# Attention, routing and a mixture of experts on one core: expert 0's first weights loaded and halved earlier, routing marks dealt anew

## Chip, core and metric

The kernel runs on one core of one Trainium2 chip. The metric is the device time of one execution in microseconds (us), the median of several. The core's engines are TensorE (PE for matmuls, PEld for weight loads), VectorE (DVE), ScalarE (ACT), GpSimd (POOL) and SyncE (SP), which here only issues DMAs.

## What is computed

Attention over 4 batches, 8 heads, 768 positions and 64 dimensions, where a query sees the first 8 positions and the last 96; then a layer of 8 experts in which each of the 3072 tokens goes to its best two.

```python
scores = scale * q @ k.T + bias            # bias: -slope * distance
scores = where(keep, scores, -1e9)         # keep: first 8 keys, or 0 <= distance < 96
a = exp(scores - max) / (sum + 1e-9);  x = (a @ v) as 3072 tokens x 512
noisy = x @ w_gate + log1p(exp(x @ w_noise)) * noise
top2 = the two best of 8 experts;  weights = softmax over the two
for e in range(8):                         # w1[e]: 512 x 1024, w2[e]: 1024 x 512
    out[tokens of e] += weight * (relu(x @ w1[e]) @ w2[e])
```

## The kernel before

Nothing reorders the instructions: each engine runs its queue in the order in which the code issues it, so the order of the code is the schedule.

**Attention.** There are 24 blocks of 128 tokens (NT), and four pairs of heads in each, so 96 pairs (NPAIR). The loop runs over `n` in steps of two: one iteration handles two pairs, two iterations a block. In iteration `n` VectorE and ScalarE make the softmax of pairs n+2 and n+3 (`score`, L723 and L726), TensorE transposes pairs n and n+1 (`trans`, L738), then computes the score products of pairs n+4 and n+5 (`product`, 16 matmuls at L709, into two PSUM banks that `score(n+2)` has to have read), VectorE normalises pairs n-4 and n-3 (`norm`, L770 to L773), and TensorE multiplies by v (`attend(n-2)`, 32 matmuls at L759). Every second iteration `gate_t` (L321) turns a finished block for the gate; `gate_l` (L340) and `gate_s` (L355) compute its logits. At the end of an iteration `tick()` advances the routing, and then the entries of a table `todo`, filled by `at(n, f, ...)`, are run: DMA loads ahead of use, zeroing of the output, `load_w` (DMA of an expert weight piece into one of four `raw` buffers) and `split`, which halves a weight piece into a high part (ScalarE copy, L194) and a low part (a subtraction, L195; on GpSimd for expert 0's w1, on VectorE elsewhere).

**Routing.** `route(r)` is a generator for one of five segments of blocks (`SEG`: 6, 6, 5, 4 and 3 blocks). It goes through some 25 small VectorE steps (L392 to L491), one or more TensorE products for the running counts (L462 to L466), and then the marks: for every block a tile `m` of two masks (L505, a compare of 128 x 128 each) and a tile of two products `c` (L509, 128 x 168 each). TensorE multiplies the marks (L523, six matmuls for three blocks) and VectorE adds the result to the table of token positions (`tab`, L525). A bare `yield` is a step; `yield True` ends the turn. `tick()` gives every active segment up to 7 steps in each iteration, and segment 2 (`CLOSE`) up to 9. Only one of segments 0 to 2 may be marking at a time. When segment 2 is done, the list of expert 0's first 512 tokens is known (`ids0`, L233 and L234) and GpSimd issues four `gather`s of their rows (L225).

**Between attention and experts.** The last pairs are finished, `turn(0, t)` for t = 0 to 3 transposes the gathered rows (L290), copies the high part (ScalarE, L292) and subtracts it for the low part (VectorE, L293). Then `up(0, f)` for eight f multiplies expert 0's w1 with these 512 tokens (L982, 12 matmuls each; the first one needs all four turned tiles). After every third of its matmuls `ahead()` runs one slot of the table `slots`, which brings segments 3 (`late`) and 4 (`last`) up to the step count given there. Their marks must be in the table before the ranking of the experts and the other experts' gathers. From the first `down` (L1012) on come the experts.

Lines that the change touches: `marks` and its loop (L498 to L526), `tick` (L678 to L685), the `at` table (L875 to L881), the end of the attention loop and the turns (L906 to L931), and `slots` (L1062 to L1071).

Of the kernel before, what the change touches and what calls it, by code (L numbers as in the profile page):

```python
# [17 lines left out]
OP = mybir.AluOpType  # L18
# [16 lines left out]
def tile_local_global_attention_then_moe(  # L35
# [348 lines left out]
    def route(r):  # L384
# [110 lines left out]
        groups = [range(i, min(i + size, w)) for i in range(0, w, size)]  # L495
        put_in = {}

        def marks(i):  # L498

            eng = nc.vector if r >= CLOSE else nc.gpsimd  # L500
            m = wts.tile([P, 2, P], FR, name="m", bufs=5)
            b = gp.tile([P, Dm], F32, name="xg", bufs=5)
            c = b[:, :6 * E * TT].bitcast(FR).rearrange("p (j x t) -> p j x t", j=2, t=TT)
            for j in range(2):
                eng.tensor_scalar(m[:, j], iota_p, row[:, i, j:j + 1], None, op0=OP.is_equal)  # L505
            cs = [P, 3 * E, TT]
            for j in range(2):
                what = ev[:, i, j].rearrange("p x e -> p (x e)")[:, :, None]
                eng.tensor_tensor(c[:, j], what.to_broadcast(cs), band[:, i, j][:, None, :].to_broadcast(cs), op=OP.mult)  # L509
            put_in[i] = m, c  # L510

        while r <= CLOSE and marking:
            yield True
        marking.append(r)
        for x, gr in enumerate(groups):
            for i in gr:
                marks(i)
                yield from (None, ) if r <= CLOSE else (None, ) * 3
            yield from (True, ) * (1 + (r < CLOSE)) if r <= CLOSE else (None, ) * 3
            ps = lgp[:, (SW + 1) * E:][:, :3 * E * TT]  # L520
            m = [(m[:, j], c[:, j]) for i in gr for m, c in [put_in.pop(i)] for j in range(2)]
            for k, (l, o) in enumerate(m):
                nc.tensor.matmul(ps, l, o, start=k == 0, stop=k == len(m) - 1)  # L523
            yield from some(2)
            nc.vector.tensor_add(tab, tab, ps.rearrange("p (x e t) -> p x e t", x=3, e=E))  # L525
            yield  # L526
# [16 lines left out]
    with ExitStack() as actx:  # L543
# [133 lines left out]

        def tick():  # L678

            for x in active[:]:  # L680
                n, v = 9 if x[1] == CLOSE else 7, None
                while n and v is None:
                    v = next(x[0], 0)
                    n -= 1
                if v == 0:  # L685
                    active.remove(x)

# [173 lines left out]
        else:  # L861
# [11 lines left out]
                    for k in range(NBH):  # L873
                        at(n + 4 * k, load_qk, *divmod(g // NBH + 1, 2), k)
            for j in range(NZ):  # L875
                at(58 + 5 * j, zero_out, j)
            for j in range(NU):
                at(84 + j // 2 * 4, load_w)
                at(36 + 4 * j, load_w)
            for j in range(FC):  # L880
                at(48 + 4 * j, split, 0, 1, j // 2 + j % 2 * NU, nc.gpsimd)  # L881
            ends = [z - 1 for a, z in SEG]


# [4 lines left out]
            for n in range(0, NPAIR, 2):  # L889
                g, odd = divmod(n // 2 - LAG, 2)  # L890
                if n + 2 < NPAIR:
                    score(n + 2)
                trans(n)
                trans(n + 1)
                if g >= 0:
                    if odd:
                        gate_s(g)
                        if g in ends:
                            active.append((Steps(route(ends.index(g))), ends.index(g)))
                    else:  # L900
                        gate_t(g)
                if n + 4 < NPAIR:
                    product(n + 4)
                if n >= 4:
                    norm(n - 4)
                if n == NPAIR - 2:  # L906
                    gate_t(NT - 2)
                if n >= 2:
                    attend(n - 2)
                if g >= 0 and not odd:  # L910
                    gate_l(g)
                if n < NPAIR - 2:
                    tick()
                for x in n, n + 1:
                    for f, a in todo.pop(x, []):
                        f(*a)
# [5 lines left out]
            norm(NPAIR - 4)  # L922
            norm(NPAIR - 2)
            gate_l(NT - 2)
            tick()
            for t in range(TA):
                if t == 2:
                    gate_s(NT - 2)
                turn(0, t, bank("m" if t == 2 else "sc"))
                if t % 2:  # L930
                    tick()  # L931
            routes[NT - 1] = route(len(SEG) - 1)
            assert len(routes) == 1 and not todo
            pending = [x for x, _ in active] + [Steps(x) for x in routes.values()]
# [3 lines left out]
    with ExitStack() as mctx:  # L938
# [109 lines left out]
        def back(e, i):  # L1048
# [11 lines left out]

        late, last = pending
        slots = {  # L1062
            0: [(late, 30)], 1: [gate_t, (late, 34)], 2: [(late, 38)], 3: [gate_l, (late, 41)],
            4: [(late, 43)], 5: [gate_s, (late, 45)], 6: [(last, 2)], 7: [(late, 48)],
            8: [(last, 5)], 9: [(last, 7)], 10: [(late, 52), (last, 8)], 11: [(last, 9)],
            12: [(last, 12)], 13: [(late, 54), (last, 13)], 14: [(last, 16)], 15: [(last, 18)],
            16: [(last, 20)], 17: [(last, 22)], 18: [(last, 24)], 19: [(last, 27)],
            20: [(last, 31)], 21: [(late, 57)], 22: [(last, 34)], 23: [(last, 37)],
            24: [(last, 39)], 25: [(last, 42)], 26: [(late, 61)], 27: [(last, 45)],
            28: [(last, 48)], 29: [(late, 99), split], 30: [split], 31: [(last, 52)],  # L1070
        }  # L1071
# [382 lines left out]
```

## Time and profile before

| | us |
|---|---|
| median of 3 runs | 749.58 (748.22 to 752.47) |
| the profiled execution | 745.59 |
| its span, first to last instruction | 743.8 |

| engine | busy, us | share of the span |
|---|---|---|
| PE | 715.6 | 96% |
| PEld | 642.2 | 86% |
| DVE | 459.3 | 62% |
| ACT | 398.3 | 54% |
| POOL | 278.9 | 37% |

The busy share is an average over stages. It says which engine is the bound most of the time, and it takes the slices of the span to see where that engine stands still. A matmul's time depends on the granted clock of TensorE, which has two levels here, 1.0 (2.4 GHz) and 0.5 (1.2 GHz); a mean between them says for what part of a stretch the lower one held.

### The profile page before, as it was taken

How to read it: one execution, taken by the hardware profiler on the slowest of the kernel's cores; microseconds unless marked ns; L12 is line 12 of the kernel's file. 1: busy time of each engine (PE TensorE's matmuls, PEld its weight loads, DVE VectorE, ACT ScalarE, POOL GpSimd, SP SyncE). 2: the span in 40 equal slices, each digit the busy share in tenths (PEclk: the TensorE clock that was granted, in tenths of full speed). 3: DMA queues.
4: the chain of work that ended last, by engine and by line, in shares of the span. 5: the costliest groups of instructions: out<-in, count | busy, mean ns of one | idle time of the engine just before them, and what ended most of it. 6: DMA issues, size and time to landing. Idle time of an engine off the chain costs nothing.

```text
span 743.8 us, 16176 instructions
## 1 busy us (share of the span) xinstructions
PE 715.6 (96%) x5873; PEld 642.2 (86%) x5873; DVE 459.3 (62%) x1459; ACT 398.3 (54%) x901; POOL 278.9 (37%) x306
## 2 busy tenths in 40 slices
PE   6999998987999999999999999999999999999994
PEld 5888886876889999999999998999899899889983
DVE  6669696867856567736664674576276657637500
ACT  6787886652324466546554654565455546436510
POOL 2000828020056083164515552652545345532231
PEclk9999999898999999999999999999999999999998
DMA  8988978555065065155625463463447444642233
GB/s 230 305 249 245 282 249 280 179 180 219 0 175 162 1 133 156 33 98 146 140 53 117 127 130 58 100 146 97 73 127 170 63 109 131 127 68 87 30 44 44
DMA packets 84392, 99.74 MB, mean 134 GB/s; under 512 B 6100, under 2 KB 51284, under 8 KB 84304
## 3 DMA queue, kind: packets, MB, share of 16 engines
q1 hardware_dynamic: 73040, 72.79, 31.8%
q0 software_dynamic: 11264, 25.83, 19.8%
q8 instruction: 48, 0.79, 0.4%
q14 instruction: 40, 0.33, 0.1%
HBM read 71.01 MB, written 27.59 MB: 133 GB/s over the span
## 4 chain that ended last, share of the span: by engine, by line
PE 80%; DVE 7%; issue 5%; POOL 3%; ACT 2%; DMA 1%; POOLq 0%; SPq 0%; ACTq 0%; DVEq 0%
PE av L1012 23%; PE bank L1265 22%; PE av L1035 9%; PE av L759 6%; PE sc L709 4%; PE at L738 4%; PE at L982 3%; PE bank L1157 2%; PE sc L982 2%; POOL out_dram L993 2%; DVE wall L195 1%; PE m L321 1%; DVE ns L723 1%; PE m L340 1%; PE bank L1058 1%
## 5 line engine op out<-in xcount | busy, mean ns | idle before, releaser
L1265 PE MATMUL bank<-xh,wall 128*128 128x384 f32 (+4 forms) x784 | 215.5, 342 | 0.8 <-DVE aside L1298 0.6
L1265 PEld LDWEIGHTS bank<-xh,wall 128*128 128x128 f32 x784 | 143.4, 188 | 5.6 <-DVE wall L195 1.3
L1265 PE MATMUL bank<-xl,wall 128*128 128x384 f32 (+4 forms) x392 | 133.3, 340 | 0.0
L993 POOL DMA_INDIRECT out_dram<-y,ids x40 | 63.1, 1579 | 155.4 <-ACT y L992 124.1
L1012 PE MATMUL av<-w2h,hh 128*128 128x512 f32 x304 | 120.6, 397 | 0.0
L1012 PE MATMUL av<-w2h,hl 128*128 128x512 f32 x304 | 119.4, 393 | 0.0
L1012 PE MATMUL av<-w2l,hh 128*128 128x512 f32 x304 | 119.4, 393 | 0.0
L195 DVE TENSOR_TENSOR wall<-raw,wall 128x512 fp32r<-128x512 f32 (+1 forms) x84 | 72.7, 872 | 50.2 <-ACT wall L194 50.1
L225 POOL DMA_INDIRECT xg<-xd,ids x53 | 56.8, 1071 | 87.9 <-DVE place L245 42.3
L969 DVE SCALAR_TENSOR_TENSOR hl<-bank,hh 128x384 fp32r<-128x384 f32 (+4 forms) x84 | 47.1, 560 | 61.8 <-ACT hh L965 61.7
L194 ACT ACTIVATE wall<-raw 128x512 fp32r<-128x512 f32 (+1 forms) x84 | 58.1, 700 | 46.2 <-POOL raw L1120 46.2
L726 ACT ACTIVATE a<-ns,mx 128x168 f32<-128x168 f32 (+1 forms) x192 | 66.7, 419 | 27.2 <-DVE mx L723 27.0
L1265 PEld LDWEIGHTS bank<-xl,wall 128*128 128x128 f32 x392 | 73.9, 188 | 2.6
L965 ACT ACTIVATE hh<-bank 128x384 fp32r<-128x384 f32 (+4 forms) x84 | 41.6, 495 | 58.5 <-DVE bank L1333 40.1
L1012 PEld LDWEIGHTS av<-w2h,hl 128*128 128x128 f32 x304 | 57.1, 188 | 12.7
L723 DVE CUSTOM_DVE_ANT_0 ns<-sc,bias 128x168 f32<-128x168 f32 (+1 forms) x192 | 50.9, 320 | 23.7 <-PE sc L709 16.3
L1012 PEld LDWEIGHTS av<-w2h,hh 128*128 128x128 f32 x304 | 57.1, 188 | 9.6 <-ACT aside L1044 0.2
L1012 PEld LDWEIGHTS av<-w2l,hh 128*128 128x128 f32 x304 | 57.1, 188 | 9.5 <-DVE w2l L195 0.3
L759 PE MATMUL av<-vs,at 128*64 128x65 f32 (+1 forms) x768 | 58.8, 228 | 0.0
L709 PE MATMUL sc<-ks,qbuf 64*64 64x168 f32 (+1 forms) x768 | 43.8, 326 | 12.3 <-DMA qbuf<-in_q 4.7
L759 PEld LDWEIGHTS av<-vs,at 128*64 128x64 f32 (+1 forms) x768 | 52.4, 139 | 2.3 <-issue 1.8
L1119 POOL TENSOR_TENSOR raw<-raw 128x256 f32<-128x256 f32 x28 | 22.4, 798 | 81.6 <-DVE wall L195 81.3
(214 smaller groups left out, 1440.8 us busy)
## 6 DMA issues: line engine op xcount, KB each, us to landing
raw<-in_w SPq DMA_DIRECT2D x64, 256.0 KB
raw<-in_w SPq DMA_DIRECT2D x32, 512.0 KB
out_dram<-zero SPq DMA_DIRECT2D x14, 512.0 KB
vs<-in_v SPq DMA_DIRECT2D x24, 260.0 KB
qbuf<-in_q SPq DMA_DIRECT2D x24, 256.0 KB
xd<-y SPq DMA_DIRECT2D x24, 256.0 KB
ks<-in_k SPq DMA_DIRECT2D x20, 272.0 KB
vp<-in_v SPq DMA_DIRECT2D x20, 195.0 KB
```

The source lines that it names most:

```text
L194: nc.scalar.activation(hi, src, AF.Copy)
L195: eng.tensor_sub(lo, src, hi.bitcast(F32))
L225: nc.gpsimd.indirect_dma_start(out=xg[e, t], out_offset=None, in_=xd[:n], in_offset=bass.IndirectOffsetOnAxis(ap=r, axis=0), bounds_check= ...
L709: nc.tensor.matmul(SC[n + x][y * Q:(y + 1) * Q, s], qs[b, j][r, 2 * i0 + s, u + y], ks[b, j][r, u + y, k0:k0 + w], start=True, stop=True, ...
L723: nc.vector.tensor_tensor_reduce(out=ns[x][:, s, :w], in0=ps[:, s], in1=bias[:, u + x, s] if i else bias0[:, u + x, s], scale=-scale, scal ...
L726: nc.scalar.activation(A[n + x][:, s * w:(s + 1) * w], ns[x][:, s, :w], AF.Exp, bias=mx[x][:, s:s + 1], scale=-1.0)
L759: nc.tensor.matmul(ps[s * Q:(s + 1) * Q, h], a[r:z, part * P + q0:part * P + q0 + Q], t[r:z, c], start=k == 0 and (n == 1 or h == 0), stop ...
L969: nc.vector.scalar_tensor_tensor(lo, src, 0.0, hi.bitcast(F32), op0=OP.max, op1=OP.subtract)
L993: ins = nc.gpsimd.indirect_dma_start(out=out, out_offset=bass.IndirectOffsetOnAxis(ap=r, axis=0), in_=y, in_offset=None, bounds_check=N + ...
L1012: nc.tensor.matmul(ps, x[j][:, f, cols], w[:, f], start=n == 0, stop=n == 3 * FC - 1)
L1035: nc.tensor.matmul(to, w[:, f, cols], x[:, f], start=n == 0, stop=n == 3 * FC - 1)
L1265: nc.tensor.matmul(ps, wb[c % 2][u][:, 2 * a + k], x[v][:, 2 * b + k], start=start and n == 0, stop=stop and n == 5, skip_group_check=True)
```

## The change

Four things are done.

1. Expert 0's w1 is loaded by `load_w` at n = 8, 10, 12, 14 (before: 36, 40, 44, 48) and halved by `split` at n = 16, 18, ... 30 (before: 48, 52, ... 76). Zeroing of the output starts at n = 63 and comes every 4 pairs (before: 58, every 5).
2. The masks are taken out of `marks` into `mask`. For segments 0, 1 and 2 GpSimd makes them, all of a group ahead of its products; for segments 3 and 4 VectorE makes them. The products run on VectorE for all segments. Before, GpSimd made masks and products of segments 0 and 1, VectorE those of 2, 3 and 4.
3. A block's products count as three steps in segments 0 to 2 (`yield 3`), a group of marks ends with one `True`, and `tick` gives 10 steps to segment 2, 3 steps to segments 0 and 1 while segment 2 is active, and 7 otherwise.
4. One more `tick()` is run in the last iteration. The four turns follow each other with no tick between them; one `gate_s` and one tick come after them (before: one tick ahead of the turns, one after the second, one after the fourth). `slots` has smaller steps for segment 3 and other ones for segment 4.

```diff
+        def mask(i):
+            m = wts.tile([P, 2, P], FR, name="m", bufs=5)
+            for j in range(2):
+                (nc.vector if r > CLOSE else nc.gpsimd).tensor_scalar(m[:, j], iota_p, row[:, i, j:j + 1], None,
+                                                                      op0=OP.is_equal)
+            put_in[i] = m
+
         def marks(i):
-            eng = nc.vector if r >= CLOSE else nc.gpsimd
-            m = wts.tile([P, 2, P], FR, name="m", bufs=5)
...
-            for j in range(2):
-                eng.tensor_scalar(m[:, j], iota_p, row[:, i, j:j + 1], None, op0=OP.is_equal)
...
-                eng.tensor_tensor(c[:, j], what.to_broadcast(cs), band[:, i, j][:, None, :].to_broadcast(cs), op=OP.mult)
+                nc.vector.tensor_tensor(c[:, j], what.to_broadcast(cs),
+                                        band[:, i, j][:, None, :].to_broadcast(cs), op=OP.mult)
...
         for x, gr in enumerate(groups):
+            if r <= CLOSE:
+                for i in gr:
+                    mask(i)
             for i in gr:
+                if r > CLOSE:
+                    mask(i)
                 marks(i)
-                yield from (None, ) if r <= CLOSE else (None, ) * 3
-            yield from (True, ) * (1 + (r < CLOSE)) if r <= CLOSE else (None, ) * 3
+                yield from (3, ) if r <= CLOSE else (None, ) * 3
+            yield from (True, ) if r <= CLOSE else (None, ) * 3
...
+            close = CLOSE in [x[1] for x in active]
             for x in active[:]:
-                n, v = 9 if x[1] == CLOSE else 7, None
-                while n and v is None:
+                n, v = 10 if x[1] == CLOSE else 3 if close and x[1] < CLOSE else 7, None
+                while n > 0 and v not in (0, True):
                     v = next(x[0], 0)
-                    n -= 1
+                    n -= 3 if v == 3 else 1
...
-                at(58 + 5 * j, zero_out, j)
+                at(63 + 4 * j, zero_out, j)
...
-                at(36 + 4 * j, load_w)
+                at(8 + 2 * j, load_w)
...
-                at(48 + 4 * j, split, 0, 1, j // 2 + j % 2 * NU, nc.gpsimd)
+                at(16 + 2 * j, split, 0, 1, j // 2 + j % 2 * NU, nc.gpsimd)
...
                 if n == NPAIR - 2:
                     gate_t(NT - 2)
+                    tick()
...
+            for t in range(TA):
+                turn(0, t, bank("m" if t == 2 else "sc"))
+            gate_s(NT - 2)
             tick()
-            for t in range(TA):
-                if t == 2:
-                    gate_s(NT - 2)
-                turn(0, t, bank("m" if t == 2 else "sc"))
-                if t % 2:
-                    tick()
...
-            0: [(late, 30)], 1: [gate_t, (late, 34)], 2: [(late, 38)], 3: [gate_l, (late, 41)],
+            0: [(late, 24)], 1: [gate_t, (late, 27)], 2: [(late, 30)], 3: [gate_l, (late, 33)],
```

On GpSimd, from the last constants to the first gather, before: masks (L505), products (L509) and the subtractions of w1's split (L195) alternate; three of the places where they meet are shown.

```order
L195 TENSOR_TENSOR xl<-raw,xh 128x4x128 x4
L505 TENSOR_SCALAR wall<-iota_p,aside 128x128 x2
L509 TENSOR_TENSOR xg<-aside 128x168 x2
...
L195 TENSOR_TENSOR xl<-raw,xh 128x4x128 x2
...
L195 TENSOR_TENSOR xl<-raw,xh 128x4x128
L225 DMA xg<-xd,ids_87 128x512 x4
```

The same stretch of GpSimd's queue now, whole (the masks are at L501):

```order
L678 MEMSET zero 128x512
L195 TENSOR_TENSOR xl<-raw,xh 128x4x128 x8
L501 TENSOR_SCALAR wall<-iota_p,aside 128x128 x34
L225 DMA xg<-xd,ids_87 128x512 x4
```

All eight subtractions now stand ahead of the first mask, the 24 products are gone, and 34 masks are left, ten more than before.

On VectorE, the turn of iteration n = 76, between the end of one `norm` (L773, now L782) and the next `score` (L723, now L732), before: the addition of segment 1's first marks and segment 2's first long steps.

```order
L773 TENSOR_TENSOR y_97<-av,den 128x256
L525 TENSOR_TENSOR tab<-tab,lg 128x168
L397 TENSOR_SCALAR aside<-aside 128x40
L399 RECIPROCAL aside<-aside 128x40
L401 TENSOR_TENSOR aside<-aside 128x40
L403 TENSOR_TENSOR aside<-aside 128x40
L405 TENSOR_SCALAR aside<-aside 128x40
L408 SCALAR_TENSOR_TENSOR aside<-aside 128x40 x4
L723 ISA ns,mx<-sc,bias 128x168
```

The same turn now:

```order
L782 TENSOR_TENSOR y_97<-av,den 128x256
L511 TENSOR_TENSOR xg<-aside 128x168 x2
L397 TENSOR_SCALAR aside<-aside 128x40
L399 RECIPROCAL aside<-aside 128x40
L401 TENSOR_TENSOR aside<-aside 128x40
L403 TENSOR_TENSOR aside<-aside 128x40
L405 TENSOR_SCALAR aside<-aside 128x40
L408 SCALAR_TENSOR_TENSOR aside<-aside 128x40 x5
L732 ISA ns,mx<-sc,bias 128x168
```

Two of segment 1's products and one more L408 stand in it; the addition to the table moved one iteration ahead. The turn of n = 78 holds two products more and two more pairs of L422 and L424, and one L408 less.

On VectorE, the turn of iteration n = 86, where segment 2 makes its marks, before (the block of two masks and two products stands five times):

```order
L491 TENSOR_TENSOR aside<-aside,first 128x70
L505 TENSOR_SCALAR wall<-iota_p,aside 128x128 x2
L509 TENSOR_TENSOR xg<-aside 128x168 x2
...
L509 TENSOR_TENSOR xg<-aside 128x168 x2
L723 ISA ns,mx<-sc,bias 128x168
```

and now, over the turns of n = 86 and n = 88:

```order
L491 TENSOR_TENSOR aside<-aside,first 128x70
L511 TENSOR_TENSOR xg<-aside 128x168 x6
L732 ISA ns,mx<-sc,bias 128x168
...
L782 TENSOR_TENSOR y_98<-av,den 128x256
L511 TENSOR_TENSOR xg<-aside 128x168 x4
L732 ISA ns,mx<-sc,bias 128x168
```

The ten masks are gone from VectorE, and the ten products are in two turns. TensorE's ten matmuls on these marks come one iteration later than before, behind the last score product and one `attend`.

## Rows read from the trace of the kernel before

**Rows 1.** The page's busy tenths of TensorE in 40 slices of 18.6 us.

```profile
PE   6999998987999999999999999999999999999994
```

**Rows 2.** Busy time by stretch: stretch, length, then busy us (instructions) of each engine, TensorE's clock, DMA.

```profile
74.63:109.03 34.40, 34.40 (x654) 29.87 (x654) 27.80 (x175) 28.72 (x82) 18.67 (x29) 1.00 0.87 265
112.08:124.53 12.45, 12.43 (x234) 10.61 (x233) 6.95 (x45) 9.51 (x29) 10.71 (x18) 1.00 0.94 304
124.53:159.99 35.46, 29.00 (x434) 24.73 (x435) 27.83 (x159) 20.13 (x56) 5.54 (x10) 0.86 0.58 196
175.62:203.56 27.94, 27.94 (x140) 22.54 (x137) 21.39 (x103) 7.18 (x15) 0.00 (x0) 0.90 0.10 35
```

**Rows 3.** Timeline of TensorE: start, length, instruction, idle time before it and its releaser.

```profile
130.77 1.61 PE L709 MATMUL sc<-ks,qbuf 64*64 64x168 f32 x13 [3.48 <-DVE mx L723]
...
153.24 0.47 PE L709 MATMUL sc<-ks,qbuf 64*64 64x168 f32 x2 [2.82 <-issue]
```

**Rows 4.** Timeline of GpSimd and VectorE, iteration n = 76.

```profile
126.77 1.18 POOL L505 TENSOR_SCALAR wall<-iota_p,aside 128x128 fp32r<-128x128 f32 x2
127.91 0.93 POOL L509 TENSOR_TENSOR xg<-aside 128x168 fp32r<-128x168 f32 x2
128.81 1.26 POOL L195 TENSOR_TENSOR xl<-raw,xh 128x512 fp32r<-128x512 f32 x1
...
126.84 0.35 DVE L401 TENSOR_TENSOR aside<-aside 128x40 f32<-128x40 f32 x1
127.78 0.20 DVE L408 SCALAR_TENSOR_TENSOR aside<-aside 128x40 f32<-128x40 f32 x1
...
127.78 2.34 DVE L408 SCALAR_TENSOR_TENSOR aside<-aside 128x40 f32<-128x40 f32 x4
130.04 0.32 DVE L723 CUSTOM_DVE_ANT_0 ns<-sc,bias 128x168 f32<-128x168 f32 x1
```

**Rows 5.** Timeline of VectorE, the same steps with GpSimd idle.

```profile
131.79 0.42 DVE L408 SCALAR_TENSOR_TENSOR aside<-aside 128x40 f32<-128x40 f32 x2
...
162.94 0.19 DVE L397 TENSOR_SCALAR aside<-aside 128x32 f32<-128x32 f32 x1
...
163.56 0.19 DVE L401 TENSOR_TENSOR aside<-aside 128x32 f32<-128x32 f32 x1
```

**Rows 6.** Timeline of VectorE, segment 2's marks, n = 86.

```profile
148.16 0.47 DVE L505 TENSOR_SCALAR wall<-iota_p,aside 128x128 fp32r<-128x128 f32 x2
148.56 0.57 DVE L509 TENSOR_TENSOR xg<-aside 128x168 fp32r<-128x168 f32 x2
...
152.56 0.32 DVE L723 CUSTOM_DVE_ANT_0 ns<-sc,bias 128x168 f32<-128x168 f32 x1
```

**Rows 7.** Chain of waits, then timelines of several engines, marks to the first expert matmul.

```profile
136.93 0.73 PE sc L709 x16
137.66 1.08 PE av L759 x32
...
157.76 1.28 PE lg L523 x10
...
160.10 0.33 DVE L525 TENSOR_TENSOR tab<-tab,lg 128x168 f32<-128x168 f32 x1 [2.15 <-PE lg L355]
161.87 1.29 POOL L225 DMA_INDIRECT xg<-xd,ids  x1 [31.80 <-issue]
171.58 0.63 PE L290 MATMUL sc<-ident,xg 128*128 128x128 f32 x4 [0.81 <-DMA xg<-xd,ids]
173.19 0.58 ACT L292 ACTIVATE wall<-m 128x512 fp32r<-128x512 f32 x1
175.62 0.77 PE L982 MATMUL at<-wall,xh 128*128 128x512 f32 x1
```

**Rows 8.** Busy time by stretch, columns as in rows 2, where weights come and where they came.

```profile
19.40:32.00 12.60, 12.47 (x236) 10.63 (x235) 7.83 (x50) 9.45 (x27) 1.77 (x7) 1.00 1.03 316
...
60.00:84.00 24.00, 23.91 (x471) 20.68 (x469) 19.14 (x132) 19.71 (x56) 8.20 (x15) 1.00 0.96 280
```

More of the change, by code (lines that the diff above doesn't have):

```diff
@@ L508, in marks @@
                 what = ev[:, i, j].rearrange("p x e -> p (x e)")[:, :, None]
-                eng.tensor_tensor(c[:, j], what.to_broadcast(cs), band[:, i, j][:, None, :].to_broadcast(cs), op=OP.mult)
-            put_in[i] = m, c
+                nc.vector.tensor_tensor(c[:, j], what.to_broadcast(cs),
+                                        band[:, i, j][:, None, :].to_broadcast(cs), op=OP.mult)
+            put_in[i] = put_in[i], c
         while r <= CLOSE and marking:
@@ L1062, in tile_local_global_attention_then_moe @@
         slots = {
-            0: [(late, 30)], 1: [gate_t, (late, 34)], 2: [(late, 38)], 3: [gate_l, (late, 41)],
[L1064 to L1068, printed above, removed]
+            0: [(late, 24)], 1: [gate_t, (late, 27)], 2: [(late, 30)], 3: [gate_l, (late, 33)],
+            4: [(late, 36)], 5: [gate_s, (late, 39)], 6: [(late, 42)], 7: [(late, 45), (last, 2)],
+            8: [], 9: [(late, 48), (last, 5)], 10: [(last, 7)], 11: [(last, 8)],
+            12: [(late, 52), (last, 9)], 13: [(last, 12)], 14: [(last, 14)], 15: [(late, 54), (last, 16)],
+            16: [(last, 19)], 17: [(last, 21)], 18: [(last, 23)], 19: [(last, 26)],
+            20: [(last, 30)], 21: [(last, 33)], 22: [(late, 57), (last, 35)], 23: [(last, 37)],
             24: [(last, 39)], 25: [(last, 42)], 26: [(late, 61)], 27: [(last, 45)],
```

## Prediction

> **What bounds the kernel now.** I read the slices of the span first. TensorE is busy to nine tenths in nearly every slice, so a microsecond is only to be had where it stands still; the weak slices are the eighth to the tenth, about 130 to 186 us [rows 1]. Everything behind 203.56, the experts, is TensorE work and only shifts.
>
> Next I compared two stretches of attention with the same TensorE work by their busy times [rows 2]. The eleven iterations n = 44 to 64 take 34.40 us with TensorE busy throughout at full clock: 3.13 us each. The eleven iterations n = 68 to 88 (the second and third row, to be added) take 12.45 + 35.46 = 47.91. The excess, 13.5, lies in the third row: TensorE is busy 29.00 of 35.46 us, and its mean clock is 0.86, so it ran at 1.2 GHz for 28% of the stretch, 9.9 us.
>
> The timeline of TensorE names two stops, 3.48 us ahead of 130.77 and 2.82 ahead of 153.24 [rows 3], both at the score product, which waits until VectorE has read the banks. So VectorE's turn sets the pace there. Two things make it long. In n = 76 four L408 take 2.34 us, where two take 0.42 otherwise. The first of the four, beside GpSimd's masks, takes 0.20; the others fall beside GpSimd's products and its split subtraction, and the last one lets VectorE go on at 130.04, when that subtraction ends (128.81 + 1.26) [rows 4, 5]. In n = 86 segment 2's five blocks of masks and products hold VectorE from 148.16 to 152.56, 4.40 us [rows 6].
>
> **The change part by part.**
>
> *GpSimd's two-input work leaves the neighbourhood of the routing.* All splits are done ahead of the first mask, and no products are left on GpSimd. The L408 row says what beside such work is lost, some 1.4 us in n = 76 alone; and with it goes most of the first stop.
>
> *What VectorE gets.* Without disturbance a score with its norm takes 131.79 - 130.04 = 1.75 us [rows 4, 5], which leaves 1.38 of an iteration's 3.13. A small step is about 0.22, and L397 and L399 together take 163.56 - 162.94 = 0.62 [rows 5]. A block of two masks and two products takes 4.40/5 = 0.88, of which the masks take 148.56 - 148.16 = 0.40 and the products 0.48 [rows 6]. The turns that run over are then three:
> - n = 76: two products 0.48, L397 and L399 0.62, eight steps (L401 to L405 and five L408) 1.76: 2.86, against 1.38: 1.48 over.
> - n = 78: two products 0.48, five steps 1.10, four pairs of L422 and L424 at 0.22 each, 0.88: 2.46, 1.08 over.
> - n = 86: one step and six products, 0.22 + 1.44 = 1.66, 0.28 over.
>
> Other turns with products (segment 0's and 1's, and n = 88 with 0.96) stay under 1.38, and TensorE hides them. In sum 2.84. Beside GpSimd's masks a two-input step took 0.35 once (L401, 0.19 alone) and 0.20 once (no loss) [rows 4, 5], so each product may lose 0 to 0.16; I take 0.08, nearer to neither, for the ten products of these three turns: 0.8. The 3.6 us in sum lie on the path. If VectorE's lag is taken up by the two banks in between, it is zero.
>
> *The stretch.* 34.40 + 3.6 = 38.0 instead of 47.91. With stops of 1.5 us at most I expect no fall of the clock, since the two falls in the third row came with stops of 3.48 and 2.82 [rows 2, 3]. The last score product then starts at 112.08 + 38.0 = 150.1 instead of 159.99.
>
> *Marks and gathers.* Segment 2's ten matmuls on the marks now follow that product and one attend: 0.73 + 1.08 + 1.28 [rows 7], end at 153.2. GpSimd's ten masks take ten times 0.59 (1.18 for two [rows 4]), 5.9 us; they need only a step of n = 84, three iterations or 9.4 us earlier, so they hide. The addition to the table follows at about 153.4; from it to the first gather 161.87 - 160.10 = 1.77 us, and from there to the fourth row's transposes, which wait for its DMA, 171.58 - 161.87 = 9.71 [rows 7]: 164.9. The gathers bound this part, since TensorE has less than that left of attention.
>
> *The turns.* Before, from the fourth transposes to the first expert matmul 4.04 us passed (171.58 to 175.62), because ScalarE's copy of the third tile did not start until 173.19 [rows 7]: it stood behind a routing step that waited for VectorE. Without ticks between the turns only the fourth tile is left: 0.63, a copy of 0.58 and a subtraction of some 0.7 (an estimate: two such pairs took 175.62 - 173.19 = 2.43), 2.0 with the hand-overs. The first expert matmul at 166.9, that is 8.7 earlier.
>
> *The routing behind it.* Seven steps of segment 3 that ran between the turns while TensorE stood, at 0.22 each 1.5 us, now fall into the stretch of `up`, where VectorE was busy 21.39 of 27.94 us [rows 2]. If its idle time takes it all, it costs nothing, otherwise 1.5; I take the middle, 0.7. The low clock at the start of that stretch (mean 0.90, 20% at 1.2 GHz [rows 2]) I leave as it is: TensorE still waits for the gathers ahead of it.
>
> *The early load.* 2.1 MB come into 19.4 to 32, where the DMA engines are full already, 1.03 at 316 GB/s [rows 8]. At that rate it delays what is queued behind it by 6.6 us. Loads of k and q are issued three blocks ahead and used four iterations later, 12.5 us, so this should hide; the same bytes came in at 60 to 84 with DMA at 0.96 and TensorE busy 23.91 of 24.00 [rows 8]. ScalarE's half of the splits now comes in each iteration rather than in every second one; it is busy 28.72 of 34.40 with five of them in the stretch [rows 2], so I put 0.5 on all of this, between 0 and 6.6.
>
> *Sum.* -8.7 + 0.7 + 0.5 = -7.5. Against the profiled execution: 745.59 - 7.5 = 738.1. The median lies 3.99 above that execution, so I forecast 742.1.
>
> **The rivals.**
>
> *VectorE's lag is absorbed* (0.16). The stretch takes 34.40, 3.6 less: 738.5. For it: VectorE's turns before n = 76 are short and the banks give some lead. Against: the product waits at once in the two rows of stops.
>
> *The clock falls all the same* (0.14). Two long turns follow each other, n = 76 and 78, and TensorE would idle in 2.6 of 9 us. 3.4 to 6.8 us at 1.2 GHz, in the measure of the 9.9 in the third row [rows 2], cost half of that: 743.8 to 745.5.
>
> *The early load starves attention* (0.08). If the lead is used up, the 6.6 us come back in whole: 748.7.
>
> *VectorE waits for GpSimd's masks* (0.08), the side on which it gets slower. GpSimd now has 34 masks of 0.59, 20 us, right beside VectorE's products. Were each product held for the length of a mask, as the L408s were held by L509 and L195, the 20 us less the room of the short turns (some 3 us) would come on top: 742.1 + 17 = 759. It gets slower than before by half a per cent once a mask holds VectorE for a third of a microsecond on average (11.3 us over 34 masks). Against it: the L408 that ran beside a mask took 0.20, as alone [rows 4, 5]; for it, the 0.35 of L401. At a half of it, 750.6, the gain is eaten up. Beside this stands the Trainium skill, page "SBUF — State Buffer", section "Who interferes with whom": a VectorE instruction with two SBUF inputs contends with any GpSimd instruction that reads SBUF, and whoever comes first holds the shared port pair for its whole length. By that rule the masks, which read SBUF, would block the products and the time would be that rival's; the row of the first L408 speaks against it, the rows of the other three agree with it.
>
> *The change does not bring the marks earlier* (0.04). If segment 2's masks come late on GpSimd, the gathers are late by as much, and the time is about as before.
>
> **How the numbers follow.** The forecast has 0.50: 742.1, by itself 739.5 to 745. A measurement of this kernel tells half a per cent (3.75 us) from no change, so faster means under 745.83, slower over 753.33. Faster: 0.50 + 0.16 + 0.11 of the falling clock: 0.77. Slower: most of the full blocking by masks and an early starvation that also drops the clock, 0.05. The rest, 0.18, is the same. The range reaches from the absorbed lag with a quieter `up`, 737.5, to the early starvation in whole, 749.0; outside lie about 0.1 above and 0.08 below.
>
> **What would show it.** Of the changed kernel: no TensorE stop over 2 us between 112 and 155, clock 1.0 there; L408 at 0.2 each everywhere; the first expert matmul near 167; VectorE's products beside masks at 0.24 to 0.32 each; TensorE busy throughout 20 to 60. It is wrong if the products take 0.5 and more beside masks, if TensorE waits for k or q at 30 to 50, or if `up` shows TensorE waiting for routing matmuls or for the low half of w2.

## The result, and the profile after

| | before | after |
|---|---|---|
| median, us | 749.8 (748.22 to 752.47, 4 runs) | 742.19 (740.75 to 744.42, 4 runs) |
| profiled execution | 745.59 | 742.15 |
| a second trace of before | 749.36 | |

The ratio is 0.9898, with a 95% interval of 0.986 to 0.9935: 7.6 us faster, where 742.1 was forecast. That the total fits is no proof of its terms, and here the profile warns: from the first trace of before to the trace after only 3.4 us are won, since that execution of before lay 4 us under its median. The second trace of before (first experiment) lies at the median. The two agree to 0.2 us up to the product of n = 90 and differ behind it. So the terms are compared with the second trace, and the first is named where it differs.

The weak slices 8 to 10 of TensorE [rows 1] are gone from the page of after:

```profile
PE   7999999999999999999999999999999999999993
```

A stretch "n = a to b" runs from the first score product of iteration a to that of the iteration after b. Busy time by stretch, columns as in [rows 2]; first of the kernel after (n = 44 to 64, 68 to 88, to the first expert matmul, `up`), then of the second trace of before (n = 68 to 88, to the first expert matmul, `up`):

```profile
76.23:112.62 36.39, 35.61 (x654) 30.28 (x654) 29.92 (x189) 26.91 (x78) 7.52 (x12) 1.00 0.69 209
115.67:154.44 38.77, 36.94 (x657) 31.69 (x657) 34.01 (x203) 26.24 (x77) 14.28 (x22) 0.96 0.88 274
154.44:172.52 18.08, 15.75 (x204) 12.92 (x203) 9.46 (x44) 8.30 (x21) 4.31 (x4) 0.81 0.56 200
172.52:199.81 27.29, 26.69 (x147) 20.90 (x148) 23.67 (x126) 7.20 (x16) 0.00 (x0) 1.00 0.18 67
```

```profile
112.27:160.18 47.91, 41.42 (x667) 35.37 (x667) 34.78 (x203) 29.64 (x84) 16.22 (x27) 0.89 0.68 223
160.18:180.58 20.40, 14.44 (x207) 11.74 (x207) 12.38 (x67) 7.32 (x18) 4.30 (x4) 0.83 0.62 216
180.58:207.39 26.81, 26.81 (x139) 21.62 (x137) 21.27 (x103) 7.01 (x14) 0.00 (x0) 0.94 0.08 28
```

| stretch | forecast | first trace to after | second trace to after |
|---|---|---|---|
| start to n = 44 | +0.5 (early load, all of it) | +1.6 | +1.4 |
| n = 44 to 66 | 0 | +2.0 | +2.0 |
| n = 68 to 88 | -9.9 | -9.1 | -9.1 |
| last score product to first expert matmul | +1.2 | +2.5 | -2.3 |
| `up` | +0.7 | -0.7 | +0.5 |
| sum | -7.5 | -3.7 | -7.6 |

The spans differ by 3.4 and 7.2 us; what the sums leave over lies in the experts, some 540 us in every trace. The stretch n = 68 to 88 did what was forecast, to 0.8 us; two terms ahead of it were missed, and the tail moved by an amount that depends on which trace of before one holds it against.

### The profile page after: what moved, and what is told of

Same layout as the page of the kernel before. It is cut to its first block, busy times and chain, and to the rows that moved or that the text cites. A ratio compares the mean times of both kernels' runs of the same rounds, so it can differ in the third digit from the quotient of the medians.

```text
span 740.4 us, 16172 instructions
## 1 busy us (share of the span) xinstructions
PE 716.3 (97%) x5873; PEld 641.1 (87%) x5873; DVE 460.3 (62%) x1473; ACT 397.4 (54%) x901; POOL 275.6 (37%) x292
## 4 chain that ended last, share of the span: by engine, by line
PE 80%; DVE 6%; issue 6%; POOL 2%; ACT 2%; DMA 2%; SPq 0%; POOLq 0%; ACTq 0%; DVEq 0%
PE av L1019 23%; PE bank L1272 22%; PE av L1042 9%; PE av L768 6%; PE sc L718 5%; PE at L747 4%; PE bank L1164 2%; PE at L989 2%; PE sc L989 2%; POOL out_dram L1000 2%; DVE wall L195 1%; PE m L321 1%; PE m L340 1%; DMA qbuf<-in_q 1%; PE bank L1065 1%
## 5 line engine op out<-in xcount | busy, mean ns | idle before, releaser
L195 DVE TENSOR_TENSOR wall<-raw,wall 128x512 fp32r<-128x512 f32 (+1 forms) x84 | 72.7, 872 | 50.5 <-ACT wall L194 50.4
L194 ACT ACTIVATE wall<-raw 128x512 fp32r<-128x512 f32 (+1 forms) x84 | 58.1, 700 | 46.6 <-POOL raw L1127 46.6
L732 DVE CUSTOM_DVE_ANT_0 ns<-sc,bias 128x168 f32<-128x168 f32 (+1 forms) x192 | 50.8, 321 | 14.2 <-PE sc L718 8.3
```

The costliest lines, as they stand in the source:

```text
L194: nc.scalar.activation(hi, src, AF.Copy)
L195: eng.tensor_sub(lo, src, hi.bitcast(F32))
L732: nc.vector.tensor_tensor_reduce(out=ns[x][:, s, :w], in0=ps[:, s], in1=bias[:, u + x, s] if i else bias0[:, u + x, s], scale=-scale, scal ...
```

## Experiments

All times of before here and below are of the same chip as the run beside them: 750.0 us in the first group of runs, 749.9 in the second (from the change without the early load to the zeros sooner), 745.8 (a pair counted as one step, both edits, nine steps) and 747.5 (all zeros out of the tail) on the two chips of the last ones. Ratios are therefore what can be compared between groups, with care: no trace of before was taken on those two chips, so it is not known what makes it faster there. A traced execution can also lie off its own median: by +2.5 us for the early load alone (750.9) and by -2.7 for the youngest segment first (736.77), by 1.2 at most for the other edited kernels. What is read from the tails of those two traces holds for these executions.

**Before, traced again.** Nothing is edited.

> The kernel before, unchanged, for a second trace. The first trace's execution took 745.59 us where the timed runs had a median of 749.6, and the changed kernel's trace was no faster than its own timed runs, so the two traces differ by 3.4 us and the medians by 7.6. If the first trace was simply a fast execution, this one lies near 749 and shows where the 4 us are (more of the span at the lower TensorE clock, or longer stops near 130 and 153 us). If tracing itself takes something away, this one lies near 745.6 again, while the timed runs beside it lie near 749.

749.36 us. In the tail VectorE's `den` waits 2.39 us, and ScalarE 3.6, for something that the trace does not name; TensorE stops for 2.56 us, and a stretch of low clock follows (0.83 above, where the first trace has 0.96 from 160.00 to 175.62). Timelines of VectorE and TensorE, second trace:

```profile
164.42 0.42 DVE L408 SCALAR_TENSOR_TENSOR aside<-aside 128x32 f32<-128x32 f32 x2
167.23 0.16 DVE L770 TENSOR_SCALAR den<-av 128x4 f32<-128x4 f32 x1 [2.39 <-remote]
```

```profile
168.12 0.69 PE L321 MATMUL m<-ident,y 128*128 128x128 f32 x2 [2.56 <-DVE y L773]
180.23 0.19 PE L462 MATMUL lg<-aside,upper 128*128 128x8 bf16 x2 [3.27 <-DVE aside L439]
```

The first trace has neither the 2.39 nor the 2.56. On this chip, where before takes 750.0, it is the exception: the first expert matmul stands at 175.62 there and at 180.58 here.

**The three parts alone.** Each kernel is before with one part of the change.

```diff
-                at(58 + 5 * j, zero_out, j)
+                at(63 + 4 * j, zero_out, j)
...
-                at(36 + 4 * j, load_w)
+                at(8 + 2 * j, load_w)
...
-                at(48 + 4 * j, split, 0, 1, j // 2 + j % 2 * NU, nc.gpsimd)
+                at(16 + 2 * j, split, 0, 1, j // 2 + j % 2 * NU, nc.gpsimd)
```

> Only the early load and halving of expert 0's w1 (and the later zeroing); masks, products, ticks, turns and slots as before. Theory A (VectorE's steps are held by GpSimd's two-input work of both kinds, products and split subtractions, and by segment 2's marks): the last of the four L408 in n = 76 is no longer held, about 1 us less at that stop, segment 0's first steps are now held by the last splits (+1), the stop near 153 stays: 748 to 750. Theory B (the early load alone frees GpSimd and the DMA engines, and the marks only ride along): most of the whole gain, 742 to 744.

748.36 us, ratio 0.9984 (0.9961 to 1.0006). n = 44 comes at 76.35 instead of 74.82. The stop ahead of n = 78 falls from 3.48 [rows 3] to 1.43 us, and n = 76 and 78 from 12.3 to 9.3 us, since no halving is left beside the routing there; in this trace 3 us are given back in the tail, 30.12 us at a mean clock of 0.72 from n = 88 to the first expert matmul, where it was 27.14 at 0.81. As the execution lies 2.5 us over its median, that loss is not shown to be the usual one.

The marks alone (masks apart, products on VectorE, the new counts of `tick`):

> Only the new masks and products and the step counts of the tick; load, halving, turns and slots as before. Theory A: the stop near 153 goes (4.4 us of marks become 1.7 and 1.0), the stop near 130 shrinks but splits still hold some steps; the new wait of L392 behind the matmuls on the marks at n = 54 and n = 90 costs some 2 us each: 744 to 747. Theory B: 749 to 750.

747.56 us, ratio 0.9969 (0.9957 to 0.9982), between the two ranges. n = 86 and 88 fall from 12.74 to 6.93 us, but n = 44 to 66 grows from 37.45 to 41.76, with a stop of 1.66 us, and the stop before n = 78 is still 3.06: the halvings now run on GpSimd right beside the products and the steps.

The tail alone (a tick more, turns in a row, new slots):

> Only the turns without ticks between them, the extra tick of the last iteration and the new slots. Theory A: ScalarE's third copy no longer waits for the routing, the first expert matmul comes 2 us earlier and the stretch of the first expert product is 0 to 1 us longer: 747.5 to 749. Theory B: no change from this, 749 to 750.

746.86 us, ratio 0.9962 (0.9947 to 0.9978), a little better than theory A. The tail from n = 88 to the first expert matmul falls from 27.15 to 24.36: the 3.27 us before L462 are gone, the 2.5 behind `den` stay.

The three gains, 1.6, 2.4 and 3.1 us, add to some 7.2, the whole change gives 7.6. The first is not clear of noise by itself: its interval reaches 1.0006.

**The change without the early load.** The undo of one part:

> The changed kernel with expert 0's load, its halving and the zero fill put back where they stood before; the marks on VectorE and the new order of the tail stay. Theory (the earlier halving loses 1.4 us before n=44, but without it the halving's GpSimd work lies in n=48 to 76 beside the masks, and there the marks wait for it; in the run with the marks alone n=44 to 66 took 41.76 and n=68 to 88 37.24 us, against 39.44 and 34.89 with both): 742.2 - 1.4 + 2.3 + 2.35 = 745.4 us (744.5 to 746.5). Rival (the parts add up, and the early load is worth the 1.6 us that it gave alone): 743.8 us. If the early load only costs: 740.8 us.

743.9 us, ratio 0.9925 (0.9897 to 0.9953), against 742.19 with it. The rival, that the parts add up, was right, though the intervals of the two ratios overlap and the 1.7 us by themselves are not clear of noise. Both stretches lost what was expected (41.75 us in n = 44 to 66 and 37.24 in n = 68 to 86, in place of 39.44 and 34.89), but the start to n = 44 won 2.0, not 1.4. Its VectorE and GpSimd, and then VectorE of the kernel after, show what the early halving avoids, in the turn of n = 76:

```profile
131.04 2.10 DVE L408 SCALAR_TENSOR_TENSOR aside<-aside 128x40 f32<-128x40 f32 x5
```

```profile
126.50 3.91 POOL L501 TENSOR_SCALAR wall<-iota_p,aside 128x128 fp32r<-128x128 f32 x6
130.89 1.26 POOL L195 TENSOR_TENSOR xl<-raw,xh 128x512 fp32r<-128x512 f32 x1 [0.47 <-ACT xh L194]
```

```profile
130.18 1.13 DVE L408 SCALAR_TENSOR_TENSOR aside<-aside 128x40 f32<-128x40 f32 x5
```

**Halvings two iterations sooner.** On the changed kernel:

```diff
-                at(16 + 2 * j, split, 0, 1, j // 2 + j % 2 * NU, nc.gpsimd)
+                at(12 + 2 * j, split, 0, 1, j // 2 + j % 2 * NU, nc.gpsimd)
```

> The changed kernel with the eight halvings of expert 0's weights each two iterations earlier (after iterations n=12 to 26, not 16 to 30). Theory (VectorE's steps of segment 0 in n=32 and n=34 take 0.90 and 1.01 us in place of 0.2 because a subtraction of the halving runs on GpSimd at the time): those two iterations fall back from 3.25 and 3.55 to 2.62 and 3.12 us, the loss at n=22 and n=28 (ScalarE's copy ahead of the attention's) only moves, and the time is about 741.1 us (740.5 to 742). Rival (the halvings find other work to hold, or wait for their load, 2.2 us of issue and the landing, and hold ScalarE's queue): 742.2 to 744 us.

741.31 us, ratio 0.9896 (0.9866 to 0.9925), as the theory said to 0.2 us. The time alone shows nothing, since the ratio of the change is 0.9898; the rows do. n = 32 and 34 fall from 3.25 and 3.55 to 2.62 and 3.12. Two steps of segment 0 on VectorE, after the change and then in this kernel:

```profile
53.54 0.90 DVE L394 SCALAR_TENSOR_TENSOR aside<-aside 128x48 f32<-128x48 f32 x1
56.11 1.01 DVE L397 TENSOR_SCALAR aside<-aside 128x48 f32<-128x48 f32 x1
```

```profile
53.91 0.21 DVE L394 SCALAR_TENSOR_TENSOR aside<-aside 128x48 f32<-128x48 f32 x1
56.23 0.18 DVE L397 TENSOR_SCALAR aside<-aside 128x48 f32<-128x48 f32 x1
```

After the change GpSimd's L195 runs from 53.09 to 54.37 and from 55.79 to 57.06, and each step ends about when it does; in this kernel the last one ends at 50.55. GpSimd after the change:

```profile
53.09 1.28 POOL L195 TENSOR_TENSOR xl<-raw,xh 128x512 fp32r<-128x512 f32 x1 [2.92 <-ACT xh L194]
55.79 1.27 POOL L195 TENSOR_TENSOR xl<-raw,xh 128x512 fp32r<-128x512 f32 x1 [1.42 <-ACT xh L194]
```

The 0.4 us at n = 22 and 28 stay, where ScalarE's copy L194 stands ahead of the attention's L330.

**The youngest segment first.** On the changed kernel:

```diff
-            for x in active[:]:
+            for x in active[::-1]:
```

> The changed kernel, but in every tick the youngest routing segment takes its steps first, so that the copy of the scores of the next segment (L392) is no longer queued on VectorE behind the subtraction that waits for the six marks' matmuls of the older one (L531). Theory (this order causes the waits of iterations n = 54 to 58, +0.80, +0.51 and +0.50 us against the second trace of before, and the 3.34 us idle of VectorE at 157.64 in the tail): the stretch n=44 to n=66 falls from 39.44 to about 37.5 us, the tail by about 1.3 us, and the time is about 739 us (737.5 to 740). Rival (the products of segment 1 are what is late, and putting them behind segment 2's steps only moves the wait into n=76 to 78): 742 us, within 1. The worst case is 745 us, if segment 1's products then hold the stop of 1.79 us before n=78 open for longer.

739.5 us, ratio 0.9871 (0.9841 to 0.9901), the lowest ratio of all, though its interval overlaps that of the change; the two runs beside it that leave the order alone took 741.3 and 741.8. n = 44 to 66 takes 37.32 us, and 37.3 in each of the three later kernels with this order. In this trace, which is the fastest of the four executions, the tail takes 19.42 in place of 21.95, and the clock stays at its upper level until 726.8 us. The view of line L531 of the kernel after says who waits for the marks' matmuls, and the timeline of VectorE where:

```profile
who waited for it (us, times):
  DVE aside L392: 6.5, 2
  POOL wall L501: 3.8, 2
```

```profile
93.96 0.26 DVE L392 COPY aside<-lg 128x96 f32<-128x96 f32 x1 [3.12 <-PE lg L531]
...
157.64 0.23 DVE L392 COPY aside<-lg 128x64 f32<-128x64 f32 x1 [3.34 <-PE lg L531]
...
159.77 0.32 DVE L533 TENSOR_TENSOR tab<-tab,lg 128x168 f32<-128x168 f32 x1
```

With the youngest first the same copies wait only for the matmuls that make their scores, L355:

```profile
91.20 0.26 DVE L392 COPY aside<-lg 128x96 f32<-128x96 f32 x1 [0.47 <-PE lg L355]
...
152.01 0.22 DVE L392 COPY aside<-lg 128x64 f32<-128x64 f32 x1 [0.18 <-PE lg L355]
...
156.23 0.32 DVE L533 TENSOR_TENSOR tab<-tab,lg 128x168 f32<-128x168 f32 x1
```

So the wait is one of order: L392 copies scores out of the tile `lg`, the marks' matmuls write another part of it, and whichever is issued first goes first. VectorE takes its queue in order, and the next score stands behind the copy.

**The zeros sooner.** The eight writes of zeros of attention at n = 36 to 64 (`at(36 + 4 * j, zero_out, j)`).

> The changed kernel with the eight writes of zeros to the output at n=36 to 64 in place of 63 to 91, so that none of them is left in the queue in the tail. Theory (the transfers of 390 GB/s beside the gathers are what delays PE's attend matmuls in the tail, 2.8 us until 167.23 on VectorE, released by something that the trace doesn't name): that wait goes, the low clock after it too, and the time is about 739 us (738 to 740.5). Rival (that wait belongs to the gathers or to something else, and the zero fill is hidden either way): 742.2 us, within 0.7. If the fill then holds back the loads of q, k and v in attention's middle: 744 us or more.

741.82 us, ratio 0.9899 (0.9868 to 0.9929), as after the change; the 2.8 us wait of `den` is still there, at 167.21. It does not come from those eight writes. Six more are issued for `up`, though, and stood in the tail as before: one is issued at 163.33, five from 169.18 on, behind that wait.

**A pair of products counted as one step** (`n -= 1` for every step).

> The changed kernel, but a pair of products counts as one step in a tick, not three, so that all three pairs of a group, six products of 0.29 us, fall into one turn. Theory (the count of three is what keeps the products under the 1.38 us that a turn's routing may take beside the scores, so without it a turn holds 6 x 0.29 = 1.75 us of products alone): three turns of segments 0 and 1 lose 0.4 to 0.8 us each, and the time is 743 to 744.5 us. Rival (the count doesn't matter for the sum, and it is the place of the marks' matmuls that does: here segment 0's last subtraction L533 stands a turn earlier and ahead of segment 1's L392, so that VectorE no longer waits there): the wait of n=54 to 58 goes, and the time is 740 to 741 us. No difference would be 742.2 us.

739.36 us, ratio 0.990 (0.9865 to 0.9935): under both expectations in us, on a chip where before is 4 us faster, and no worse than the change by the ratio, so no gain of the count of three is seen in the sum. Both theories are seen in it. Four products of segment 1 fall into the turn of n = 76, ten of segment 2 into that of n = 86; n = 78 takes 7.06 us with a stop of 2.29, and n = 88 5.24. VectorE:

```profile
127.05 1.05 DVE L511 TENSOR_TENSOR xg<-aside 128x168 fp32r<-128x168 f32 x4
...
148.40 2.89 DVE L511 TENSOR_TENSOR xg<-aside 128x168 fp32r<-128x168 f32 x10
```

n = 68 to 86 loses 2.65 us by that. But L533 now stands ahead of L392, at 92.45 and 157.24; n = 44 to 66 falls to 38.14, and the tail to 17.94 us at full clock.

**Both edits, then nine steps for segment 2.** The youngest first and the halvings sooner; then also `n, v = 9` for segment 2.

> Both edits that helped: the youngest segment's steps first in every tick, and the halvings two iterations earlier. Theory (they act in different iterations, n=20 to 34 the one, n=54 to 58 and the tail the other): 739.5 - 0.9 = 738.6 us (737.5 to 739.5), with n=32 and 34 at 2.62 and 3.12 us, n=44 to 66 in 37.3 us and no stretch of low clock before the experts' end. Rival (one absorbs the other): 739.5 us.

741.27 us, ratio 0.9935 (0.9915 to 0.9955): a miss, over theory and rival. The ratio is also made worse by the faster before of this chip.

> The same two edits, and segment 2, the one that closes the first gathers, takes nine steps in a tick as it did before the change, not ten. The turn of n=76 then has four of the polynomial's steps (0.20 to 0.23 us each) beside two products, not five, and n=78 three pieces of the search for the largest less; the ten products and their matmuls stand in the same turn as with ten. Theory (the stop of 1.79 us before n=78 is the sum of what one turn gives VectorE): that stop falls to about 1.6 us, n=76 to 82 give back 0.2 to 0.8 us together, and the time is about 738.2 us (737.5 to 739). Rival (the tenth step is needed for the last marks): the tail grows by one turn's wait, 739 to 741 us.

740.83 us, ratio 0.9931 (0.9909 to 0.9954): over the 739 us of the theory as well. Up to n = 88 both did what was expected: 147.75 and 147.46 us, against 148.07 with the youngest first alone; the nine steps brought the stop before n = 78 from 1.78 to 1.55. The tail lost it: 22.72 and 21.85 in place of 19.42, though the last comes from an execution 2.7 us under its median. TensorE now comes to the turns before the gathered rows. Timelines of TensorE at the turns, with the youngest first alone, with both edits, and with nine steps:

```profile
164.03 0.66 PE L290 MATMUL sc<-ident,xg 128*128 128x128 f32 x4 [0.40 <-DMA xg<-xd,ids]
164.74 0.63 PE L290 MATMUL m<-ident,xg 128*128 128x128 f32 x4
166.18 0.63 PE L290 MATMUL sc<-ident,xg 128*128 128x128 f32 x4 [0.81 <-DVE wall L293]
```

```profile
162.50 0.66 PE L290 MATMUL sc<-ident,xg 128*128 128x128 f32 x4 [0.93 <-DMA xg<-xd,ids]
165.34 1.12 PE L290 MATMUL sc<-ident,xg 128*128 128x128 f32 x4 [2.18 <-DMA xg<-xd,ids]
```

```profile
162.42 0.66 PE L290 MATMUL sc<-ident,xg 128*128 128x128 f32 x4 [1.16 <-DMA xg<-xd,ids]
...
167.53 1.09 PE L290 MATMUL sc<-ident,xg 128*128 128x128 f32 x4 [2.69 <-DMA xg<-xd,ids]
```

**All zeros out of the tail.** The kernel with nine steps, and all fourteen writes at n = 30 to 82.

> The kernel of the last three edits (youngest segment first, halvings two iterations earlier, nine steps for segment 2), and all fourteen writes of zeros to the output at n=30 to 82, none in the tail. In the two runs with the earlier marks the first gathers end on GpSimd by 162.9 us, but PE's turns stop for their landings (2.18 us before 165.34; 1.16 and 2.69 us before 162.42 and 167.53), while five writes of 512 KB stand on the queues from 162 us on at 390 to 410 GB/s, and 6.83 to 10.2 us of low clock follow. Theory (the gathers' 0.26 MB each share the queues with the zeros): the stops of the turns fall under 1 us, no low clock follows, the tail goes from 21.9 to about 19 us, and the time is 0.4 to 0.6 per cent under that of the run with nine steps, at a ratio to before of about 0.988, or 737.5 us where before takes 745.8 and 740.5 where it takes 749.9. Rival (the landing is the gathers' own latency, 4.4 us at the median in the first trace of before, and varies by itself): the stops stay at 2 to 3 us, and the ratio at 0.993.

739.05 us, ratio 0.9895 (0.9877 to 0.9913), between theory and rival. The data rate from 156 to 170 us fell from 295 to 114 GB/s, and the longest stop from 2.69 to 1.13:

```profile
162.70 0.66 PE L290 MATMUL sc<-ident,xg 128*128 128x128 f32 x4 [0.87 <-DMA xg<-xd,ids]
164.49 1.09 PE L290 MATMUL m<-ident,xg 128*128 128x128 f32 x4 [1.13 <-DMA xg<-xd,ids]
166.49 1.09 PE L290 MATMUL sc<-ident,xg 128*128 128x128 f32 x4 [0.92 <-DMA xg<-xd,ids]
```

But each of these three turns still waits, 2.9 us in all, and the clock still fell, for 10.2 us from 164.3 on. That the zeros delay the gathers is made likely by the longest stop and by the median from issue to landing, 4.6 us with nine steps and 4.0 here; that TensorE waits for the gathers there with or without them is shown.

## Why the prediction was right, and where it was not

**The stretch n = 68 to 88: right.** 38.0 us were forecast, 38.77 measured. The two stops of [rows 3] are gone but for one of 1.79 us before n = 78, the turn that the working named as the worst:

```profile
131.96 1.16 PE L718 MATMUL sc<-ks,qbuf 64*64 64x168 f32 x13 [1.79 <-DVE mx L732]
```

That GpSimd's two-input work was the cause of the slow steps in n = 76 is shown by the run without the early load (five L408 in 2.10 us beside L195) against the kernel after (five in 1.13), and by the halvings sooner. The clock did fall once, 3.4 us in this stretch, against the forecast of none. By the working's own measure that costs half of it, 1.7, so VectorE's lag cost some 2.7 us (38.77 - 34.40 - 1.7, an estimate) and not the 3.6 of the sum. The heading of [rows 5] is wrong for its last two rows: the first two gathers run on GpSimd beside them, from 161.87 for 1.29 us and from 163.46 for 1.01. The price of a small step stays, since 0.2 each is also what L408 takes alone.

**Products beside masks: the allowance not needed, the base too low.** Six products beside GpSimd's masks take 0.29 each, two alone 0.28. So the masks add some 0.01 where 0.08 was allowed, and a product costs 0.28, not the 0.24 of the working; the two errors nearly cancel:

```profile
145.77 6.58 POOL L501 TENSOR_SCALAR wall<-iota_p,aside 128x128 fp32r<-128x128 f32 x10 [20.20 <-PE sc L718]
```

```profile
88.17 0.56 DVE L511 TENSOR_TENSOR xg<-aside 128x168 fp32r<-128x168 f32 x2
...
147.99 1.74 DVE L511 TENSOR_TENSOR xg<-aside 128x168 fp32r<-128x168 f32 x6
```

The rival in which VectorE waits for the masks is out. The rule of the Trainium skill, "SBUF — State Buffer", "Who interferes with whom", is borne out here for GpSimd's two-input work alone (0.90 against 0.21), and not for its compares with a scalar (0.29 against 0.28).

**The early load: the term was mis-sized.** +0.5 was forecast for everything, +1.4 to 1.6 measured. TensorE waited for no load between 18 and 77 us. The first 0.4 + 0.4 us, at n = 22 and 28, is ScalarE's copy ahead of the attention's, which the working named; the 0.6 + 0.4 at n = 32 and 34 is the hold of segment 0's first steps by the last two halvings. The sentence "all splits are done ahead of the first mask" was true and not enough: they were not done ahead of the first step.

**n = 44 to 66: the step that failed.** The working let "other turns with products" stay under the room that TensorE hides. It counted what VectorE executes and not what stands at the head of its queue: L392 waits 3.12 us for matmuls that the same tick issues ahead of it, and n = 54 to 58 lose 1.8 us. The youngest segment first gives 2.1 us of that stretch back.

**Marks and gathers: one step of four failed, another came out by luck.** The marks' matmuls end 3.2 us after the last score product (3.1 forecast), the first gather stands 1.67 us behind the addition (1.77), the fourth row's transposes 9.74 behind the gather (9.71), the first expert matmul 1.34 behind those (2.0). That the 9.7 fits is luck: it was worked out as the time of the rows, but here TensorE comes to them late, after the unnamed wait of `den` (2.84 us) and at the lower clock, and doesn't wait for a row. But the addition was put directly behind the matmuls, at +0.2, and came 2.2 us after them: segment 3's L392 and a whole score and norm are ahead of it in VectorE's queue. Hence 18.08 where 16.8 was forecast. With the youngest first that stretch is 15.6, in the execution under its median. Timelines of TensorE, GpSimd, VectorE and TensorE, kernel after (the copy and the addition, 157.64 and 159.77, are shown above):

```profile
156.25 1.35 PE L531 MATMUL lg<-xg,wall 128*128 128x168 f32 x10
161.44 1.28 POOL L225 DMA_INDIRECT xg<-xd,ids  x1 [9.09 <-PE at L747]
167.23 0.16 DVE L779 TENSOR_SCALAR den<-av 128x4 f32<-128x4 f32 x1 [2.84 <-remote]
171.18 0.63 PE L290 MATMUL sc<-ident,xg 128*128 128x128 f32 x4
```

**The turns: right. `up`: right in the sum, by luck.** `up` takes 27.29 us against 26.81, +0.5 where +0.7 stood. But the working left the low clock at its start as it was, and it is gone: the mean clock is 1.00, where the two traces of before have 0.90 and 0.94. Length times mean clock gives an estimate of 25.1 and 25.2 us for `up` before at full clock, so the routing that moved there costs some 2.1, above the 1.5 that the working held possible, and the clock gives 1.6 of it back.

**The base: luck.** The sum -7.5 was made against an execution whose tail was short by chance, and then lifted by 3.99 to the median. What lay in those 3.99 us was taken for something that the change leaves alone. In fact it is one stop and its low clock, in the very stretch that the change rebuilds. The kernel after has the same unnamed wait at `den` too, 2.84 us, and 6.8 us of low clock in its tail, so the change does not take that wait away. The tail was costed at +1.2 against a trace without it; measured it is +2.5 against that trace and -2.3 against the one that has the wait as well. What was won there is not that wait but, as the run with the tail alone shows, the stop of 3.27 us before L462. The forecast was right in total because the tail came out 3.5 us better, like with like, and the rest 3.5 worse (2.0 of L392, 0.9 of the early halving, 0.8 in n = 68 to 88, less 0.2 in `up`).

## What to carry to other kernels

Where a scheduler deals steps of several chains into one turn, look at the head of each in-order queue: a chain whose next step waits for something issued in the same turn goes last. Place GpSimd's two-input work where VectorE's small steps are not, to the first step and not only to the first long one. And before a sum is made against one profiled execution, trace it again if it lies under the timed runs: the difference has a place, and the change may be there. The same holds for the traces of experiments.

## What the runs showed of the hardware

The clock does not follow the longest stop alone. The kernel after fell to the lower level about 1.6 us behind its 1.79 us stop; the one with the youngest first has the same 1.79 us stop before n = 78, and its windows show 1.00 throughout:

```profile
113.45:151.20 37.75, 35.15 (x651) 29.84 (x651) 33.31 (x202) 25.41 (x75) 14.01 (x22) 1.00 0.88 274
148.07:167.49 19.42, 17.43 (x269) 13.97 (x268) 13.33 (x65) 11.25 (x29) 5.63 (x7) 1.00 0.68 225
```

With all zeros out of the tail, three stops of about 1 us within 4.7 us came with 10.2 us of it, and the same kernel's stop of 1.54 us before n = 78 with 3.4 us, while the run with nine steps has 1.55 us there and no fall. What else decides stays open here.

The wait for something unnamed at the same `den` stays open as well. It is 2.2 to 2.4 us in three of the four traces with the old marks (the first one lacks it), and 2.8 to 4.3 in the five with the new marks and the old order of the segments. It is in none of the five traces where L392 no longer waits for the marks' matmuls (youngest first, or a pair counted as one step); the first gather begins at 157.3 to 158.9 us there, and at 161.44 after the change. So the order may take it away, which would be part of what the youngest first wins in the tail; no run shows what the wait is for. The four gathers on GpSimd run beside it, but no run took them away.
